# A softmax attention kernel: the exponential's [128,1] bias operand taken out, and its offset moved elsewhere

## The chip, the cores and the metric

The kernel runs on one core of one Trainium2 chip. The metric is the device time of one execution in microseconds (us); lower is better. Executions of one kernel mostly agree within 0.8%. The profile also records a granted clock, the share of its full clock that the matrix engine got. A run over 1.5% above the fastest of its kernel counts as slow and is left out of comparisons. The experiments ran on two chips, on which the kernel before took 1018.94 us (b1, a1 to a3) and 1017.3 to 1017.7 us (the rest). The engines are called as the profile calls them: PE (matrix engine; PEld is its weight loads), ACT (ScalarE), DVE (VectorE), POOL and SP.

## The reference

Two attentions over the same input are mixed by a gate. A is full softmax attention: 2048 tokens, 32 heads of 20. B looks at 8 dilated positions. The part that matters here is A's softmax:

```python
scores = jnp.einsum("bhqd,bhkd->bhqk", q, k) * scale
p = _softmax(scores, axis=-1)          # 32 heads x 2048 x 2048 exponentials
o = jnp.einsum("bhqk,bhkd->bhqd", p, v)
...
return g * a + (1 - g) * b
```

That is 134 million exponentials, by far the largest piece of elementwise work. Inputs and outputs are bfloat16.

## The kernel before

Scores come out of the matmul already scaled to "128 per octave": a score of 128 n means 2 to the n. A row of the query tile carries an offset for each query, so that the largest score of a row lies below a fixed top. Before the change that offset is 128 x (127 + TOP) with TOP = 96. The 127 is the bias of a float's exponent: VectorE builds some of the exponentials by writing integers that are read as bfloat16, and there it is wanted. ScalarE does not want it, and takes it off again with the bias of its activation, which is given as a [128,1] tile.

```python
T("dve", 0.06, lambda e: e.memset(ebias[:, :], -127.0 * LN2), writes=["ebias"])
T("dve", 0.06, lambda e: e.tensor_scalar(offs[:, :], onesrow[:, :], 128.0 * (127 + TOP), None, op0=ALU.mult), ...)
...                                             # ScalarE's way, 792 tiles of 1536 and 1024 in turn
def exp(s):
    n = len(tiles[s])                           # 3 or 2 blocks of 512 scores
    exps[s] = T("act", actc(512 * n), lambda e: e.activation(
        ebuf[s % NE][:, 0:512 * n], score[s % 2][:, 0:512 * n], ACTF.Exp, scale=LN2 / 128.0, bias=ebias[:, 0:1]),
      reads=[("score", s % 2), "ebias"], writes=[("ebuf", s % NE)])
...                                             # VectorE's way, 68 blocks of 512: four passes
T("dve", dvc(512), lambda e, b=b: e.tensor_scalar(xD[w][:, :], side[b][:, :], 16384.0, None, op0=ALU.max), ...)
T("dve", ...)  # tD = (n - 2^16) n, with n the low 16 bits of xD
T("dve", ...)  # tD = (n + H1) tD
T("dve", ...)  # eD as integers = H2 tD + xD
```

The order of all instructions is fixed when the program is built, by a planner that holds estimates of durations (`actc(n)` is 0.08 us plus 0.83 ns an element, `dvc(n)` is 0.10 us plus 1.04 ns an element). And where PE would be idle, the planner inserts matmuls whose results nobody uses ("fillers"), to keep PE's clock up:

```python
def filler(limit):
    while sch.avail["pe"] + 0.32 <= limit and sch.load(2.3) < FILL:
        ...
        T("pe", 0.215, lambda e: e.matmul(obank[:, :], zero[:, :], xT[:, 0, 0:512], start=False, stop=False, ...), ...)
```

There are two score buffers. The score matmuls of tile s may start when the exponential of tile s-2 has ended, and must be done when that of tile s-1 ends.

Of the kernel before, what the change touches and what calls it, by code (L numbers as in the profile page):

```python
# [5 lines left out]
FP32 = mybir.dt.float32  # L6
# [4 lines left out]
ALU = mybir.AluOpType  # L11
ACTF = mybir.ActivationFunctionType
AX = mybir.AxisListType

P = 128
# [12 lines left out]
SCALE = float(DH) ** -0.5  # L28
NEG = -1.0e9
TOK = 256  # L30



# [3 lines left out]
LN2 = 0.6931471805599453  # L37
OCT = 128.0 * SCALE / LN2
TOP = 96
# [175 lines left out]
def bass_gated_mix__softmax_full_mha__sliding_local_dilated__prompt_kernel(  # L215
    nc,
    A_x,
    A_wqkv,
    A_wo,
    B_x,  # L220
    B_wqkv,
    B_wo,
    gate_w,
    out,
):
    from contextlib import ExitStack

    with ExitStack() as ctx:
        _build(ctx, nc, A_x, A_wqkv, A_wo, B_wqkv, B_wo, gate_w, out)
# [10 lines left out]
def _build(ctx, nc, A_x, A_wqkv, A_wo, B_wqkv, B_wo, gate_w, out):  # L240
    sb = lambda shape, dt, name: ctx.enter_context(nc.sbuf_tensor(name, shape, dt))
# [3 lines left out]
    T = sch.task  # L245
# [3 lines left out]
    score = [ps(512 * TSZ[0], "score0"), ps(512 * TSZ[1], "score1")]  # L249
    obank = ps(512, "obank")  # L250
    side = [ps(512, "side0"), ps(512, "side1")]


    NE = 6
# [9 lines left out]
    ebuf = [sb([P, 512 * TSZ[i % 2]], BF16, "ebuf%d" % i) for i in range(NE)]  # L264
# [9 lines left out]
    xD = [gtan, gtr]  # L274
    ND = 4
    eD = sb([P, ND, 512], BF16, "eD")
    tD = sb([P, 512], FP32, "tD")
    ebias = sb([P, 1], FP32, "ebias")
    offs = sb([P, 1], FP32, "offs")
    g16 = sb([P, 16], FP32, "g16")  # L280
    tB = sb([P, TOK], FP32, "tB")
    gwT = sb([P, CN], BF16, "gwT")
# [6 lines left out]
    onesrow = sb([P, 1], FP32, "onesrow")  # L289
    qB = sb([P, CN, TOK], BF16, "qB")  # L290
    kB = sb([P, CN, TOK + PADB], BF16, "kB")
    vB = sb([P, CN, TOK + PADB], BF16, "vB")
    stage = sb([P, WIN * CN * TOK], BF16, "stage")
    eB = sb([P, 2 * TOK], BF16, "eB")
    mB = sb([P, TOK], BF16, "mB")
# [26 lines left out]
    dvc = lambda n, mode=1: 0.10 + n * 1.0417e-3 / mode  # L322
# [6 lines left out]
    def x_load(tcc, dur):  # L329
# [12 lines left out]
      writes=["WvA"], dma=True)  # L342
    T("sp", 14.0, lambda e: e.dma_start(_ap(stage, 0, [[2 * D, CN], [1, 2 * D]]), wA_v[:, :, 0:2 * D]),
      writes=["stage"], dma=True)
# [2 lines left out]

    T("pool", 0.3, lambda e: e.iota(itmp[:, :], [[1, P]], base=0, channel_multiplier=-1), writes=["itmp"])
    T("dve", 0.06, lambda e: e.memset(warm[:, :], 0.0), writes=["warm"])
    T("dve", 0.06, lambda e: e.memset(ebias[:, :], -127.0 * LN2), writes=["ebias"])  # L350
    T("act", 1.4, lambda e: e.activation(warm[:, 2:4], warm[:, 0:2], ACTF.Exp), reads=["warm"], writes=["warm2"])
    T("dve", 0.2, lambda e: e.memset(qabs[:, :], 0.0), writes=["qabs"])

# [2 lines left out]
      reads=["rB"], writes=["ident"])  # L356
    T("dve", 0.1, lambda e: e.memset(zero[:, :], 0.0), writes=["zero"])

    for i in range(7):
# [7 lines left out]
      reads=["warm"], writes=["WkP1"])  # L367
# [4 lines left out]
    for j in range(4):  # L372
        T("dve", 0.07, lambda e, j=j: e.memset(onesrow[32 * j:32 * j + 1, :], 1.0), writes=["onesrow"])
        T("dve", 0.1, lambda e, j=j: e.memset(KMmask[32 * j:32 * j + 32, 32 * j:32 * j + 1], -1.0078125),
          writes=["KMmask"])


    T("dve", 0.06, lambda e: e.tensor_scalar(offs[:, :], onesrow[:, :], 128.0 * (127 + TOP), None, op0=ALU.mult),
      reads=["onesrow"], writes=["offs"])

    def constants():
# [41 lines left out]
    def bank():  # L423
        while True:
            got = yield ("bank",)
            if got is not None:
                return got

    def release(b, t):
        bank_used[b] = False  # L430
        bank_free[b] = t.end + LAT[t.stream]
# [135 lines left out]
    def gen_d(w):  # L567


        while True:  # L570
            while lock[w] or not wanted():
                yield ("cond",)
            lock[w] = True
            b = yield from bank()
            it = yield ("ride", b)
            if it is None:
                it = lone(b)
            i, g, kb, j = it
            sl = (4 * i + j) % ND
            yield ("dve", DAHEAD)  # L580
            t = T("dve", dvc(512), lambda e, b=b: e.tensor_scalar(xD[w][:, :], side[b][:, :], 16384.0, None, op0=ALU.max),
                  reads=[("side", b)], writes=[("xD", w)])
            release(b, t)
            nn = xD[w][:, :].bitcast(U16)[:, 0:1024:2]
            while lock[2]:
                yield ("cond",)
            lock[2] = True
            yield ("dve", DAHEAD)
            T("dve", dvc(512), lambda e, nn=nn: e.scalar_tensor_tensor(tD[:, :], nn, -OCT16, nn, op0=ALU.add, op1=ALU.mult),
              reads=[("xD", w)], writes=["tD"])  # L590
            yield ("dve", DAHEAD)
            T("dve", dvc(512), lambda e, nn=nn: e.scalar_tensor_tensor(tD[:, :], nn, H1, tD[:, :], op0=ALU.add, op1=ALU.mult),  # L592
              reads=[("xD", w), "tD"], writes=["tD"])
            yield ("dve", DAHEAD)
            T("dve", dvc(512), lambda e, sl=sl: e.scalar_tensor_tensor(  # L595
                eD[:, sl, :].bitcast(I16), tD[:, :], H2, xD[w][:, :], op0=ALU.mult, op1=ALU.add),
              reads=[("xD", w), "tD"], writes=[("eD", sl)])
            lock[2] = False
            lock[w] = False
            done[("du", i, j)] = True  # L600
# [361 lines left out]
    def v_first(kb0, n, s_):  # L962
# [7 lines left out]
        for i in range(n):  # L970
# [16 lines left out]
      reads=[("side", 1)], writes=["qabs"])  # L987
# [6 lines left out]
      reads=[("kmx4", i) for i in range(4)], writes=[("kmx", 0)])  # L994
    T("dve", 0.2, lambda e: e.tensor_scalar(KM[0][:, :], KMmask[:, :], kmx[:, 0:1], None, op0=ALU.mult),
      reads=[("kmx", 0), "KMmask"], writes=[("KM", 0)])
    v_first(0, 2, 1)
    T("pe", 0.215, lambda e: e.matmul(side[1][:, :], KM[0][:, :], qabs[:, :], start=False, stop=True, skip_group_check=True),
      reads=[("KM", 0), "qabs"], accum=[("side", 1)])
    t = T("dve", dvc(512), lambda e: e.tensor_scalar(qT[0][:, :], side[1][:, :], OCT, offs[:, 0:1], op0=ALU.mult, op1=ALU.add),  # L1000
          reads=[("side", 1), "offs"], writes=[("qT", 0)])
# [29 lines left out]
    def wanted():  # L1031


        if len(dopen) > waiting[0]:
            waiting[0] += 1
            return True

        if dopen or len(dquads) > cur["pv"] or not d_time():
            return False
        t_end = sch.avail["act"]  # L1040
        for g in range(cur["g"], min(NG, cur["g"] + 2)):
            lo, hi = ahead[g]
            t_end += (4 * hi - lo - 4) * UNIT
            if done.get(("q", g)) and t_end >= sch.avail["pe"] + DTIME:
                break
        else:
            return False
        ahead[g][1] = hi - 1
        dquads.append((g, hi - 1))
        dleft[g] = dleft.get(g, 0) + 4  # L1050
        dopen.extend(range(4))
        waiting[0] += 1
        return True
# [12 lines left out]
    def lone(b):  # L1066
        it = take(dopen[0])
        i, g, kb, j = it
        q = g % NQ
        T("pe", 0.215, lambda e: e.matmul(side[b][:, :], kT[32 * j:32 * j + 32, q, kb * P:(kb + 1) * P],  # L1070
                                          qT[g % 2][32 * j:32 * j + 32, :], start=True, stop=True),
          reads=[("kT", q, kb // 4), ("qT", g % 2)], writes=[("side", b)], mode="row")
        return it
# [59 lines left out]
    def exp(s):  # L1133
        n = len(tiles[s])
        exps[s] = T("act", actc(512 * n), lambda e: e.activation(  # L1135
            ebuf[s % NE][:, 0:512 * n], score[s % 2][:, 0:512 * n], ACTF.Exp, scale=LN2 / 128.0, bias=ebias[:, 0:1]),
          reads=[("score", s % 2), "ebias"], writes=[("ebuf", s % NE)])

    def pv(units, quads):

# [91 lines left out]
    s = 0  # L1232
    while pvg < NG:
# [11 lines left out]
        if acting:  # L1245
            gn = us[-1] // 64
            run_until(("q", gn))
            if gn != g1:
                g1 = gn

                if g1 + 1 < NG:
                    if g1 + 1 < NQ:
                        add_gen(gen_k(g1 + 1), 2)
                    add_gen(gen_q(g1 + 1), 2)
                if g1 == 1:
                    add_gen(gen_v(1), 3)
                    add_gen(gen_d(0), 1.0)
                    add_gen(gen_d(1), 1.01)
                if g1 == 0:
                    add_gen(gen_gate(0), 3)  # L1260
                if g1 == 2:
                    add_gen(gen_bweights(), 4)
                if g1 % NQ == 6 and g1 // NQ + 1 < QCN:
                    add_gen(gen_gate(g1 // NQ + 1), 4)
                if g1 == 4:
                    for uu in range(2 * QCN):
                        add_gen(gen_b(uu), 6 + 0.01 * uu)
                        add_gen(gen_bproj(uu), 6.5 + 0.01 * uu)
                    add_gen(gen_prefold(), 5.5)
                    for qq in range(QCN - 1):  # L1270
                        add_gen(gen_fold(qq), 5 + 0.01 * qq)
            qk(s)
            exp(s)
# [45 lines left out]
```

## Time and profile before

| | before |
|---|---|
| median time (three runs; 1019.26 with a fourth, below) | 1019.25 us |
| ACT busy | 985.6 us of 1016.0, 97% |
| of that the 792 exponentials | 971.3 us |
| ACT idle before exponentials for late scores | 10.6 us |
| PE busy | 922.8 us, 91% |
| DVE busy | 615.1 us, 61% |

The page of the kernel before: engines' busy time, the slices of the span (a digit is tenths), the chain of waits that ended last, and groups of instructions (line, engine, operation, tiles | busy us, mean ns of one | idle us before them and what ended it).

```profile
span 1016.0 us, 16619 instructions
...
PE 922.8 (91%) x6808; PEld 316.5 (31%) x6915; DVE 615.1 (61%) x1067; ACT 985.6 (97%) x827; POOL 22.9 (2%) x20
...
ACT  5989999998999999999999999999999999999996
...
PEclk9999999998999999999999999999999999999999
...
ACT 68%; issue 21%; PE 7%; DVE 3%; DMA 1%; DVEq 0%; ACTq 0%
...
L1135 ACT ACTIVATE ebuf<-score,ebias 128x1536 bf16<-128x1536 f32 (+1 forms) x792 | 971.3, 1592 | 10.8 <-PE score L1121 10.3
L1121 PE MATMUL score<-qT,kT 32*128 32x512 bf16 x1980 | 308.5, 385 | 70.4 <-ACT ebuf L1135 39.7
...
L1121 PEld LDWEIGHTS score<-qT,kT 32*128 32x128 bf16 x1980 | 75.9, 91 | 323.0 <-ACT ebuf L1135 305.4
```

ACT is busy for 80% or more of every slice but the first and last, and the chain follows it for 68% of the span. ACT stood idle before its exponentials for 10.8 us in all, 10.6 of them in waits for scores. In the other direction, the score matmuls' weight loads waited 305.4 us for an exponential. So ScalarE is the bound. PE's 91% is a warning: it is close behind.

The mean of one exponential in the group, 1592 ns, is not its cost: an activation is counted from when it is taken up, while its predecessor still runs (below, L701 starts at 508.88 and its predecessor ends at 509.32). The cost of one is the distance between the ends of two that follow each other. The timeline of ACT shows it (start in us, length in us, instructions merged in runs of one line):

```profile
505.00 4.32 ACT L1135 ACTIVATE ebuf<-score,ebias 128x1536 bf16<-128x1536 f32 x3
508.88 0.93 ACT L701 ACTIVATE eB<-side 128x512 bf16<-128x512 f32 x1
509.35 2.89 ACT L1135 ACTIVATE ebuf<-score,ebias 128x1024 bf16<-128x1024 f32 x2
511.77 0.74 ACT L713 ACTIVATE tB<-side 128x256 f32<-128x256 f32 x1
512.03 3.92 ACT L1135 ACTIVATE ebuf<-score,ebias 128x1024 bf16<-128x1024 f32 x3
```

The first run of exponentials ends at 505.00 + 4.32 = 509.32; the exponential of L701, which has no bias, ends at 508.88 + 0.93 = 509.81, so 512 elements cost 0.49 us. The next two biased ones (1024 and 1536 elements) end at 512.24, 2.43 us later; the tanh of L713, without bias and 256 wide, 0.27 us after that. From the single records, over the whole trace, the medians are 1431 ns (1536) and 1004 ns (1024) with the bias, 487 ns (512) and 273 ns (256) without. Both fit 0.833 ns an element; the fixed part is about 152 ns with the operand and 60 ns without.

For the cost of a second operation in a VectorE instruction, groups of DVE by form:

```profile
L581 DVE TENSOR_SCALAR gtan<-side 128x512 f32<-128x512 f32 x36 | 24.8, 688 | 11.9 <-PE side L1121 11.1 <-PE side L726 0.5
...
L503 DVE TENSOR_SCALAR qT<-side,offs 128x512 bf16<-128x512 f32 x31 | 23.1, 744 | 21.7 <-PE side L445 20.7 <-PE score L1121 0.9
...
L581 DVE TENSOR_SCALAR gtr<-side 128x512 f32<-128x512 f32 x32 | 21.9, 684 | 3.2 <-PE side L1121 3.2
...
L472 DVE TENSOR_SCALAR kT<-side,onesrow 128x512 bf16<-128x512 f32 x28 | 20.8, 744 | 20.8 <-PE side L445 16.6 <-PE score L1121 4.1
```

L503 multiplies and adds, L472 adds only, both with one [128,1] operand: 744 ns both.

### The profile page before, as it was taken

The numbers are of one execution on the slowest core, as the hardware profiler recorded it, in microseconds if no ns is written. First come the engines' busy times: TensorE is split into PE (matmuls) and PEld (weight loads), VectorE is DVE, ScalarE is ACT, GpSimd is POOL, SyncE is SP. The second block draws the span as 40 slices with busy tenths as digits, with TensorE's granted clock in tenths as the row PEclk, the third lists the DMA queues.
The fourth block names the chain that finished last, engine by engine and source line by source line (L and its number), as shares of the span: only waits on it lengthen the run. The fifth ranks groups of instructions, "written<-read, shape, count | busy, mean of one in ns | idle before, by whom it ended". The sixth has DMA issues, their size and how long they took to land.

```text
span 1016.0 us, 16619 instructions
## 1 busy us (share of the span) xinstructions
PE 922.8 (91%) x6808; PEld 316.5 (31%) x6915; DVE 615.1 (61%) x1067; ACT 985.6 (97%) x827; POOL 22.9 (2%) x20
## 2 busy tenths in 40 slices
PE   6989999897999999999999899999999999998997
PEld 4323222222332323233323333333332333232222
DVE  5564577788778775861664675255358326568612
ACT  5989999998999999999999999999999999999996
POOL 0000000008000000000000000000000000000000
PEclk9999999998999999999999999999999999999999
DMA  6110000020000000000000000000000000000000
GB/s 209 39 28 1 1 1 1 1 98 1 1 2 1 2 1 1 2 7 14 7 1 1 1 2 7 14 8 1 1 1 1 7 14 8 1 1 1 1 1 27
DMA packets 9769, 13.07 MB, mean 13 GB/s; under 512 B 2397, under 2 KB 8413, under 8 KB 9693
## 3 DMA queue, kind: packets, MB, share of 16 engines
q1 hardware_dynamic: 9692, 12.00, 3.6%
q8 instruction: 54, 0.88, 0.4%
q14 instruction: 23, 0.18, 0.1%
HBM read 9.38 MB, written 2.62 MB: 12 GB/s over the span
## 4 chain that ended last, share of the span: by engine, by line
ACT 68%; issue 21%; PE 7%; DVE 3%; DMA 1%; DVEq 0%; ACTq 0%
ACT ebuf L1135 67%; PE score L1121 2%; PE side L445 2%; PE obank L1165 1%; ACT tB L713 1%; DMA oTn<-in_A_x_dram 1%; PE side L948 0%; DVE qT L503 0%; PE score L930 0%; DVE eD L595 0%; ACT eB L701 0%; DVE oTt L560 0%; DVE tD L592 0%; DVE oTt L549 0%; DVE oTn L563 0%
## 5 line engine op out<-in xcount | busy, mean ns | idle before, releaser
L1135 ACT ACTIVATE ebuf<-score,ebias 128x1536 bf16<-128x1536 f32 (+1 forms) x792 | 971.3, 1592 | 10.8 <-PE score L1121 10.3
L1121 PE MATMUL score<-qT,kT 32*128 32x512 bf16 x1980 | 308.5, 385 | 70.4 <-ACT ebuf L1135 39.7
L1165 PE MATMUL obank<-ebuf,vA 128*21 128x512 bf16 x1980 | 178.2, 386 | 1.1 <-ACT ebuf L1135 1.1
L1121 PEld LDWEIGHTS score<-qT,kT 32*128 32x128 bf16 x1980 | 75.9, 91 | 323.0 <-ACT ebuf L1135 305.4
L445 PE MATMUL side<-xT,kvw 128*128 128x256 bf16 (+1 forms) x727 | 133.0, 294 | 1.0 <-issue 0.8
L1183 PE MATMUL obank<-xT,zero 128*128 128x512 bf16 x379 | 113.8, 383 | 2.9 <-issue 2.4
L445 PEld LDWEIGHTS side<-xT,kvw 128*128 128x128 bf16 x740 | 59.0, 97 | 61.8 <-issue 43.2
L1165 PEld LDWEIGHTS obank<-ebuf,vA 128*21 128x21 bf16 x1980 | 40.1, 89 | 91.6 <-issue 85.1
L846 DVE CAST outsb<-side 128x512 bf16<-128x512 f32 (+1 forms) x24 | 11.8, 490 | 72.6 <-PE side L445 72.5
L549 DVE STREAM_TRANSPOSE oTt<-obank 128x512 f32<-128x512 f32 x32 | 22.9, 716 | 49.7 <-PE obank L1165 49.2
L738 DVE TENSOR_TENSOR stage<-vB,repB 128x1280 bf16<-128x1280 bf16 x64 | 50.4, 820 | 0.8
L1183 PEld LDWEIGHTS obank<-xT,zero 128*128 128x128 bf16 x423 | 33.6, 97 | 53.8 <-issue 37.3
L660 DVE TENSOR_TENSOR stage<-qB,kB 128x1280 bf16<-128x1280 bf16 x64 | 49.1, 818 | 0.3
L445 PE MATMUL side<-woA_r,oTn 128*128 128x128 bf16 (+1 forms) x242 | 45.5, 299 | 0.4 <-issue 0.3
L445 PE MATMUL side<-stage,ident 128*128 128x512 bf16 (+1 forms) x186 | 44.7, 346 | 0.2 <-issue 0.2
L1179 PE MATMUL side<-xT,ident 128*128 128x512 bf16 x145 | 43.6, 381 | 0.7 <-issue 0.5
L445 PE MATMUL side<-xT,WqP 128*128 128x512 bf16 x139 | 42.1, 388 | 1.9 <-issue 1.0
L751 DVE SCALAR_TENSOR_TENSOR oB<-side,rB 128x512 bf16<-128x512 f32 (+1 forms) x24 | 14.4, 600 | 42.1 <-PE side L445 40.4
L503 DVE TENSOR_SCALAR qT<-side,offs 128x512 bf16<-128x512 f32 x31 | 23.1, 744 | 21.7 <-PE side L445 20.7
L495 DVE TENSOR_SCALAR qabs<-side 128x512 uint16<-128x512 uint16 x31 | 21.0, 676 | 22.8 <-PE side L445 21.4
L472 DVE TENSOR_SCALAR kT<-side,onesrow 128x512 bf16<-128x512 f32 x28 | 20.8, 744 | 20.8 <-PE side L445 16.6
L716 DVE RECIPROCAL rB<-side 128x256 f32<-128x256 f32 x8 | 14.1, 1758 | 31.6 <-ACT tB L713 31.6
(129 smaller groups left out, 750.5 us busy)
## 6 DMA issues: line engine op xcount, KB each, us to landing
stage<-in_B_wqkv_dram SPq DMA_DIRECT2D x1, 2400.0 KB, 8.5
out_dram<-outsb SPq DMA_DIRECT2D x12, 160.0 KB, 1.8
stage<-in_A_wqkv_dram SPq DMA_DIRECT2D x1, 1600.0 KB, 11.7
oTn<-in_A_x_dram SPq DMA_DIRECT2D x2, 640.0 KB, 5.7
kvw<-in_A_wqkv_dram SPq DMA_DIRECT2D x1, 800.0 KB, 8.7
woA_r<-in_A_wo_dram SPq DMA_DIRECT2D x4, 200.0 KB
woBp<-in_B_wo_dram SPq DMA_DIRECT2D x5, 160.0 KB
oB<-in_A_x_dram SPq DMA_DIRECT2D x1, 640.0 KB, 7.6
```

What stands on the lines that cost most here:

```text
L445: ins = e.matmul(o, l, r, start=(first and i == 0), stop=(last and i == n - 1), skip_group_check=True)
L472: t = T("dve", dvc(512), lambda e, b=b, tcc=tcc: e.tensor_scalar(kT[:, q, tcc * 512:(tcc + 1) * 512], side[b][:, :], onesrow[:, 0:1], None ...
L495: T("dve", dvc(512), lambda e: e.tensor_scalar(qabs[:, :].bitcast(U16), side[b][:, :].bitcast(U16)[:, 1:1024:2], 0x7FFF, None, op0=ALU.bit ...
L503: t = T("dve", dvc(512), lambda e: e.tensor_scalar(qT[sl][:, :], side[b][:, :], OCT, offs[:, 0:1], op0=ALU.mult, op1=ALU.add), reads=[("si ...
L549: T("dve", dvc(512), lambda e: e.transpose(oTt[:, :], obank[:, :]), reads=["obank"], writes=["oTt"])
L660: TB(dvc(CN * TOK, 2), lambda e, w=w, ks=ks: e.tensor_tensor(prodB(w), qB[:, :, :], ks, ALU.mult), reads=["qB", "kB"], writes=[("prod", w) ...
L738: TB(dvc(CN * TOK, 2), lambda e, w=w, vs=vs, rr=rr: e.tensor_tensor(prodB(w), vs, rr, ALU.mult), reads=["vB", ("repB", w4 % 2)], writes=[( ...
L1121: ins = e.matmul(o, kT[32 * j:32 * j + 32, q, kb * P:(kb + 1) * P], qT[g % 2][32 * j:32 * j + 32, :], start=True, stop=True)
L1135: exps[s] = T("act", actc(512 * n), lambda e: e.activation(ebuf[s % NE][:, 0:512 * n], score[s % 2][:, 0:512 * n], ACTF.Exp, scale=LN2 / 1 ...
L1165: ins = e.matmul(obank[32 * j:32 * j + DV, :], vA[:, kb, g % NQ, j, :], src, start=(kb == 0), stop=(last and k >= len(lst) - 4), skip_grou ...
L1179: t = T("pe", 0.215, lambda e, b=b: e.matmul(side[b][:, :], ident[:, :], xT[:, 0, 0:512], start=True, stop=True), reads=["ident", ("xT", 0 ...
L1183: T("pe", 0.215, lambda e: e.matmul(obank[:, :], zero[:, :], xT[:, 0, 0:512], start=False, stop=False, skip_group_check=True), reads=["zer ...
```

## The change

The offset in the query tile loses its 127, so that ScalarE needs no bias at all. VectorE adds the 127 back in its first pass, as a second operation of the same instruction.

```diff
-    ebias = sb([P, 1], FP32, "ebias")
...
-    T("dve", 0.06, lambda e: e.memset(ebias[:, :], -127.0 * LN2), writes=["ebias"])
...
-    T("dve", 0.06, lambda e: e.tensor_scalar(offs[:, :], onesrow[:, :], 128.0 * (127 + TOP), None, op0=ALU.mult),
+    T("dve", 0.06, lambda e: e.tensor_scalar(offs[:, :], onesrow[:, :], 128.0 * TOP, None, op0=ALU.mult),
       reads=["onesrow"], writes=["offs"])
...
-            t = T("dve", dvc(512), lambda e, b=b: e.tensor_scalar(xD[w][:, :], side[b][:, :], 16384.0, None, op0=ALU.max),
+            t = T("dve", dvc(512), lambda e, b=b: e.tensor_scalar(xD[w][:, :], side[b][:, :], 128.0 * 127, 16384.0, op0=ALU.add, op1=ALU.max),
...
-            ebuf[s % NE][:, 0:512 * n], score[s % 2][:, 0:512 * n], ACTF.Exp, scale=LN2 / 128.0, bias=ebias[:, 0:1]),
-          reads=[("score", s % 2), "ebias"], writes=[("ebuf", s % NE)])
+            ebuf[s % NE][:, 0:512 * n], score[s % 2][:, 0:512 * n], ACTF.Exp, scale=LN2 / 128.0),
+          reads=[("score", s % 2)], writes=[("ebuf", s % NE)])
```

The planner's estimates are not touched, so the order of instructions on every engine is the same but for the memset.

## The prediction

> **What bounds the kernel now.** ScalarE. The page gives ACT 985.6 us busy of a span of 1016.0 (97%); from 400 to 1005 us the windows view has it busy without a gap, and the chain of waits puts 67% on the exponential alone. The exponential is 792 instructions, 971.3 us by the groups. It waited for its scores only 10.6 us in all (waits of ACT), while the score matmuls' weight loads waited for it 737 times, 305 us. PE (923 us busy, 157 us of that matmuls that only keep it warm) is close behind; DVE is at 61%.
>
> **What the change does.** It takes the [128,1] bias operand from 792 exponentials. By the distance of the ends of back-to-back instructions in the trace: biased, 1536 wide 1430 ns and 1024 wide 1004 ns, which is 0.833 ns an element plus 152 ns. Exponentials and tanhs without a bias are in the same trace: 512 wide 487 ns, 256 wide 273 ns, 0.833 ns an element plus 60 ns. So a biased one pays 91 ns more. The Trainium skill, "ScalarE: Activation LUTs", section "What ACT_TABLE_LOAD costs", says that each [128,1] pointer operand adds about 93 ns; this trace agrees, at 91. 792 x 91 = 72 us of ScalarE time go; a pair of tiles (1536 + 1024) falls from 2434 to about 2252 ns.
>
> Added: a second operation in the first of four DVE passes over VectorE's 68 tiles. I expect no cost: TENSOR_SCALAR with two operations (qT, 744 ns) takes as long as with one (kT, 744 ns), both with one pointer operand; the pass stays at 684 to 690 ns. Order, tiles given to VectorE and fillers stay.
>
> **How much lies on the critical path.** Nearly all, if PE keeps up. With two score buffers, the score matmuls of tile s start 56 ns after exponential s-2 ends (nearly all 1536-wide tiles, the median of the others), and end 557 ns (1536) or 985 ns (1024, median) before ScalarE needs them. PE's own spare time before those matmuls, median, is about 140 and 40 ns, 180 a pair: just what is taken away. I carried the trace's PE work between score matmuls forward with exponentials 91 ns shorter: the last one ends 71 us earlier, with ScalarE losing about 7 us to late scores, as before, but PE's own waiting for ScalarE falls from about 100 us to about 30. So PE becomes a near second bound, and DVE results (78% busy from 230 to 400 us) that came just in time will stall PE some more; I allow 5 us.
>
> **Prediction.** 1019 - 71 + 5 = 953 us; 8 in 10 between 944 and 970. Faster by over 2%: 0.97; within 2%: 0.025; slower: 0.005.
>
> **What would show it.** Exponentials' busy sum near 900 us; ends 1339 and 913 ns apart; ACT still 95% or more of the span; waits of the score weight loads for the exponential falling far below 305 us; ScalarE's waits for score matmuls growing from 11 to 10 to 25 us; the first DVE pass unchanged near 686 ns; PE's granted clock still 0.98 or more.
>
> **What would make it wrong.** The unbiased form may not save 91 ns at 1024 and 1536 elements; PE, near saturation, may become the bound (ACT's wait for scores of 40 us or more, most of it in 230 to 400 us or around changes of head group, where PE waits for DVE's qT); a denser PE may get a lower clock. Each would leave 965 to 985 us.

## The result

The time fell from 1019.26 us (median of 4 runs, 1018.65 to 1022.91) to 954.22 us (median of 4, 950.29 to 956.01). The ratio is 0.935, 95% interval 0.9312 to 0.9387. (Ratios here are the mean time of one kernel's fast runs over that of the other's of the same rounds, so not quite the ratio of the medians.) The prediction was 953, range 944 to 970.

The page of the changed kernel; its line numbers are one lower than before:

```profile
span 954.2 us, 16618 instructions
...
PE 904.3 (95%) x6808; PEld 317.1 (33%) x6915; DVE 612.7 (64%) x1066; ACT 918.6 (96%) x827; POOL 22.9 (2%) x20
...
ACT  5979999997999999999999999999999999999996
...
PEclk8989999998999999999999999999999999999999
...
ACT 50%; PE 31%; issue 14%; DVE 4%; DMA 1%; DVEq 0%; ACTq 0%
...
L1134 ACT ACTIVATE ebuf<-score 128x1536 bf16<-128x1536 f32 (+1 forms) x792 | 902.8, 1383 | 16.0 <-PE score L1120 14.2
L1120 PE MATMUL score<-qT,kT 32*128 32x512 bf16 x1980 | 309.7, 387 | 26.5 <-ACT ebuf L1134 11.7
...
L1120 PEld LDWEIGHTS score<-qT,kT 32*128 32x128 bf16 x1980 | 76.0, 91 | 251.6 <-ACT ebuf L1134 206.7
```

The span fell by 1016.0 - 954.2 = 61.8 us. ACT's busy time fell by 985.6 - 918.6 = 67.0, nearly all of it the exponentials' (971.3 to 902.8, 68.5), and ACT's idle time rose from 30.4 to 35.6. ACT is still 96% busy, but PE is now at 95%, and the chain of waits shows the new balance: ACT 50% where it was 68%, PE 31% where it was 7%. The score weight loads' wait for the exponential went from 305.4 to 206.7 us.

ACT's timeline, around an exponential and a tanh that never had a bias:

```profile
537.22 1.68 ACT L1134 ACTIVATE ebuf<-score 128x1536 bf16<-128x1536 f32 x1
538.57 0.82 ACT L700 ACTIVATE eB<-side 128x512 bf16<-128x512 f32 x1
539.04 2.61 ACT L1134 ACTIVATE ebuf<-score 128x1024 bf16<-128x1024 f32 x2
541.27 0.65 ACT L712 ACTIVATE tB<-side 128x256 f32<-128x256 f32 x1
541.54 2.65 ACT L1134 ACTIVATE ebuf<-score 128x1024 bf16<-128x1024 f32 x2
```

The two exponentials between them end at 541.65, 2.26 us after 539.39, where two such took 2.43 before. Over the trace the medians are 1343 ns (1536) and 917 ns (1024): 88 and 87 ns less, fixed part 63 ns. 396 x (88 + 87) ns is 69 us.

VectorE's first pass, now with two operations:

```profile
L580 DVE TENSOR_SCALAR gtan<-side 128x512 f32<-128x512 f32 x36 | 24.7, 685 | 6.7 <-PE side L1120 6.4
...
L580 DVE TENSOR_SCALAR gtr<-side 128x512 f32<-128x512 f32 x32 | 21.9, 684 | 1.3 <-PE side L1120 1.2
```

684 and 685 ns where it was 684 and 688: the added operation costs nothing.

One thing in this profile was not in the other. The granted clock of this run was 0.967: 0.949 for 445 us of it. The other three runs had 0.989 to 0.994. A second look at the same kernel (below, after_again) had no such stretch, a span of 952.8 us and nearly the same ACT figures (917.0 us busy), so the low clock made no large difference and is not part of the explanation.

### The profile page after: what moved, and what is told of

Read it like the earlier page. It is cut to its first block, busy times and chain, and to the rows that moved or that the text cites. A ratio compares the mean times of both kernels' runs of the same rounds, so it can differ in the third digit from the quotient of the medians.

```text
span 954.2 us, 16618 instructions
## 1 busy us (share of the span) xinstructions
PE 904.3 (95%) x6808; PEld 317.1 (33%) x6915; DVE 612.7 (64%) x1066; ACT 918.6 (96%) x827; POOL 22.9 (2%) x20
## 4 chain that ended last, share of the span: by engine, by line
ACT 50%; PE 31%; issue 14%; DVE 4%; DMA 1%; DVEq 0%; ACTq 0%
ACT ebuf L1134 49%; PE side L444 11%; PE score L1120 9%; PE obank L1164 5%; PE obank L1182 3%; PE side L1178 1%; PE side L947 1%; DMA oTn<-in_A_x_dram 1%; DVE eD L594 0%; DVE tD L591 0%; PE score L929 0%; ACT tB L712 0%; ACT eB L700 0%; DVE qT L502 0%; DVE tD L588 0%
## 5 line engine op out<-in xcount | busy, mean ns | idle before, releaser
L1134 ACT ACTIVATE ebuf<-score 128x1536 bf16<-128x1536 f32 (+1 forms) x792 | 902.8, 1383 | 16.0 <-PE score L1120 14.2
L1120 PEld LDWEIGHTS score<-qT,kT 32*128 32x128 bf16 x1980 | 76.0, 91 | 251.6 <-ACT ebuf L1134 206.7
L444 PE MATMUL side<-xT,kvw 128*128 128x256 bf16 (+1 forms) x727 | 135.2, 298 | 1.0 <-issue 0.8
L1182 PE MATMUL obank<-xT,zero 128*128 128x512 bf16 x379 | 115.8, 389 | 2.9 <-issue 2.4
L502 DVE TENSOR_SCALAR qT<-side,offs 128x512 bf16<-128x512 f32 x31 | 23.1, 745 | 17.3 <-PE side L444 16.5
L715 DVE RECIPROCAL rB<-side 128x256 f32<-128x256 f32 x8 | 14.1, 1758 | 27.4 <-ACT tB L712 27.4
```

What stands on the lines that cost most here:

```text
L444: ins = e.matmul(o, l, r, start=(first and i == 0), stop=(last and i == n - 1), skip_group_check=True)
L502: t = T("dve", dvc(512), lambda e: e.tensor_scalar(qT[sl][:, :], side[b][:, :], OCT, offs[:, 0:1], op0=ALU.mult, op1=ALU.add), reads=[("si ...
L1120: ins = e.matmul(o, kT[32 * j:32 * j + 32, q, kb * P:(kb + 1) * P], qT[g % 2][32 * j:32 * j + 32, :], start=True, stop=True)
L1134: exps[s] = T("act", actc(512 * n), lambda e: e.activation(ebuf[s % NE][:, 0:512 * n], score[s % 2][:, 0:512 * n], ACTF.Exp, scale=LN2 / 1 ...
```

## The experiments

Two questions were put. Is it the operand that costs, or the addition, or the numbers? And how near are the other engines to being the bound now, which decides whether the rest of a saving would still arrive? All experiments gave correct results. All times are medians of fast runs unless said otherwise.

### The bias as a constant in the instruction, nothing else changed (b1_immediate_bias)

```diff
 (kernel before)
-    ..., ACTF.Exp, scale=LN2 / 128.0, bias=ebias[:, 0:1]), reads=[("score", s % 2), "ebias"],
+    ..., ACTF.Exp, scale=LN2 / 128.0, bias=-127.0 * LN2), reads=[("score", s % 2)],
```

> The kernel before, with its bias of -127 ln 2 given as a constant in the instruction instead of as a [128,1] operand; offsets and VectorE's passes stay as before. Theory 1 (the operand's fetch is the cost, not the addition): about 954 us, ends of back-to-back exponentials 1343 and 917 ns apart. Theory 2 (adding a bias that is not zero is the cost): about 1019 us, 1431 and 1004 ns. Theory 3 (the smaller numbers or the new offsets matter): about 1019 us with short exponentials or anything between. Result correct.

Measured: 952.73 us (951.84 to 953.35), ratio 0.9338, interval 0.9302 to 0.9375; ends 1344 and 916 ns apart. The group of the exponential:

```profile
L1133 ACT ACTIVATE ebuf<-score 128x1536 bf16<-128x1536 f32 (+1 forms) x792 | 901.5, 1415 | 13.1 <-PE score L1119 12.0
```

A bias that is not zero is free when it is a constant of the instruction. This falsifies theories 2 and 3: neither the addition nor the offset's size costs anything. It also means that this one-line edit gets all of the gain; moving the offset and VectorE's second operation were not needed for it.

### A bias operand of zeros put back (a1_zero_bias_operand)

```diff
 (changed kernel)
+    ebias = sb([P, 1], FP32, "ebias");  T("dve", ..., e.memset(ebias[:, :], 0.0), ...)
-    ..., ACTF.Exp, scale=LN2 / 128.0),
+    ..., ACTF.Exp, scale=LN2 / 128.0, bias=ebias[:, 0:1]),
```

> The changed kernel with a [128,1] operand of zeros put back as the exponential's bias; all else stays changed. Theory 1: back to 1016 to 1023 us, 1431 and 1004 ns between ends. Theory 2 (a bias of zero adds nothing) and theory 3 (offsets): about 954 us.

Measured: 1019.75 us (1019.54 to 1026.02), ratio 1.001, interval 0.9967 to 1.0053; ends 1431 and 1004 ns apart, as before the change.

```profile
L1136 ACT ACTIVATE ebuf<-score,ebias 128x1536 bf16<-128x1536 f32 (+1 forms) x792 | 971.5, 1590 | 11.5 <-PE score L1122 11.0
```

Adding nothing, by way of an operand, costs the whole gain.

### The scale as an operand instead (a2_scale_operand), and both (a3_both_operands)

```diff
 (changed kernel; escale is a [128,1] tile of LN2/128, ebias one of zeros)
-    ..., ACTF.Exp, scale=LN2 / 128.0),
+    ..., ACTF.Exp, scale=escale[:, 0:1]),                          (a2)
+    ..., ACTF.Exp, scale=escale[:, 0:1], bias=ebias[:, 0:1]),      (a3)
```

> The changed kernel, no bias, but the scale given as a [128,1] operand instead of a constant. Theory 1 in its wide form (any such operand costs some 87 ns an instruction): 1016 to 1023 us, 1431 and 1004 ns. Narrow form (only the bias path costs): about 954 us.

> The changed kernel with both scale and a bias of zeros as [128,1] operands. If each is fetched in turn: another 792 x 87 ns = 69 us on top of one operand, about 1088 us, 1518 and 1091 ns between ends. If the two fetches overlap: about 1019 us.

Measured: a2 1018.83 us (1017.29 to 1020.08), ratio 0.9985, ends 1431 and 1004 ns apart. a3 1090.46 us (1088.96 to 1092.31), ratio 1.0689, ends 1522 and 1095 ns apart. The group of the exponential, a2 and then a3:

```profile
L1136 ACT ACTIVATE ebuf<-score,escale 128x1536 bf16<-128x1536 f32 (+1 forms) x792 | 971.3, 1593 | 11.1 <-PE score L1122 10.6
...
L1138 ACT ACTIVATE ebuf<-score,ebias,escale 128x1536 bf16<-128x1536 f32 (+1 forms) x792 | 1043.3, 1718 | 10.2 <-PE score L1124 10.0
```

So it is not the bias path: either [128,1] operand costs 87 or 88 ns for each instruction, and the costs of two add up (88 ns for the first at 1536 elements, 91 for the second). What the engine does in that time, no record shows. The Trainium skill, "ScalarE: Activation LUTs", section "What ACT_TABLE_LOAD costs", gives about 93 ns for each [128,1] pointer operand; these runs agree within 6 ns.

### The operand on half of the exponentials (a4_bias_operand_odd_tiles)

```diff
 (changed kernel; ebias is a [128,1] tile of zeros)
-    ..., ACTF.Exp, scale=LN2 / 128.0),
+    ..., ACTF.Exp, scale=LN2 / 128.0, bias=ebias[:, 0:1] if s % 2 else 0.0),
```

Odd tiles are the 1024-wide ones. The dependency on the ebias tile is declared for all of them.

> The changed kernel with the bias operand of zeros on the 1024-wide exponentials only, half of the 792. If ScalarE bounds the kernel all the way from the time before to the time after, the response is linear: half of the 65 us lost again, 985 to 990 us. If PE's near bound had already eaten a part of the second half of the saving, less than half comes back: 970 to 984 us.

Measured: 984.37 us (983.22 to 988.02), ratio 0.9673, interval 0.9628 to 0.9717.

```profile
L1136 ACT ACTIVATE ebuf<-score 128x1536 bf16<-128x1536 f32 x396 | 677.7, 1711 | 2.2 <-PE score L1122 2.0
L1136 ACT ACTIVATE ebuf<-score,ebias 128x1024 bf16<-128x1024 f32 x396 | 544.0, 1374 | 10.5 <-PE score L1122 9.8
```

Within this one trace the 1024-wide exponentials, with the operand, end 1004 ns apart, and the 1536-wide ones, without it, 1340. So the cost stays with the instruction that has the operand, and declaring the dependency alone costs nothing. The time is 30 us over the changed kernel (31 over after_again, which ran on the same chip) and 33 us under the kernel before in the same rounds (1017.32). The expected border between the two readings was 984 to 985, so the verdict must come from the series: no, one and two operands on each exponential gave about 953, 1019 and 1090. The first operand costs 66 us and the second 71 us of time, for 69 and 72 us of ScalarE (792 x 91 ns). The response is linear where PE has room and a few us short in the last step down. ScalarE bounds the kernel over the whole range, and PE begins to take a little of the saving at its end.

### VectorE's addition as a pass of its own (a5_add_as_own_pass)

```diff
 (changed kernel; the order on PE is unchanged)
-    t = T("dve", dvc(512), ... e.tensor_scalar(xD[w], side[b], 128.0 * 127, 16384.0, op0=ALU.add, op1=ALU.max) ...)
+    t = T("dve", dvc(512), ... e.tensor_scalar(xD[w], side[b], 128.0 * 127, None, op0=ALU.add) ...)
     release(b, t)
+    T("dve", -LAT["dve"], ... e.tensor_scalar(xD[w], xD[w], 16384.0, None, op0=ALU.max) ...)   # planned as costing nothing
```

> The changed kernel with VectorE's addition as a pass of its own (from the score bank, then the maximum in place) instead of a second operation of one pass; PE's order and the plan stay. 68 more VectorE instructions of 0.4 to 0.7 us, 27 to 47 us of VectorE time. If VectorE (64% busy) has room: within 5 us of 954. If its results come just in time between 100 and 400 us, where it is over 80% busy: 960 to 975 us, with more waits of PE for it.

Measured: 973.62 us (972.62 to 973.98), ratio 0.9558: 20 us of the gain are lost. Groups of DVE by form (L583 is the new pass), then the page's chain, then ACT's waits:

```profile
L580 DVE TENSOR_SCALAR gtan<-side 128x512 f32<-128x512 f32 x36 | 24.7, 685 | 5.6 <-PE side L1122 5.4
...
L580 DVE TENSOR_SCALAR gtr<-side 128x512 f32<-128x512 f32 x32 | 21.9, 684 | 0.6 <-PE side L1122 0.5
...
L583 DVE TENSOR_SCALAR gtan<-gtan 128x512 f32<-128x512 f32 x36 | 16.5, 459 | 1.2
...
L583 DVE TENSOR_SCALAR gtr<-gtr 128x512 f32<-128x512 f32 x32 | 14.1, 440 | 1.1
```

```profile
ACT 32%; PE 29%; DVE 28%; issue 10%; DMA 0%; DVEq 0%; ACTq 0%
```

```profile
ACT ebuf L1136 <- PE score L1122: 23.9, 24, 4.5
```

The new passes are 16.5 + 14.1 = 30.6 us of an engine that is idle over a third of the time, and yet 20 us of them reach the end. The chain shows it: DVE's share is 28% where it was 4%, and ACT's waits for score matmuls rise from 14.2 to 23.9 us. In between stands PE: its own idle time that ended on a VectorE result, summed over the waits of PE, rose from 15.0 to 29.6 us. The reading is that VectorE's passes stand in the fixed order ahead of score matmuls, by the matmuls that they feed or by the banks that they free, and where they are late, PE stops; it was not followed instruction by instruction, and the sums do not account for all of the 20 us. So folding the addition into an existing pass, at no cost, was a condition of this change as it was made.

### Narrow keep-warm matmuls (a6_short_fillers, a7_fillers_384)

```diff
 (changed kernel, same order; both kinds of filler)
-    e.matmul(obank[:, :], zero[:, :], xT[:, 0, 0:512], ...)
+    e.matmul(obank[:, 0:64], zero[:, :], xT[:, 0, 0:64], ...)      (a6; 384 in place of 64 in a7)
```

> The changed kernel with the 524 matmuls that only keep PE warm shortened from 512 to 64 columns, in the same order: about 90 us of PE time go. If the losses of some 7 us that came back after the change are PE's score matmuls coming late because PE has no spare time: 946 to 950 us, ScalarE's waits near the 11 us of before. If the fillers hold the clock: more stretches at half clock (granted clock under 0.96) and 956 us or more.

> The changed kernel with the keep-warm matmuls 384 instead of 512 columns wide, same order: 28 us of PE time less. The run with 64 columns fell to half clock for 261 us and took 1012 us. If three quarters of the filler hold the clock, the late score matmuls gain: 947 to 952 us. If the clock falls already: over 960 us.

Measured: a6 took 1013.0, 1000.48 and 1010.96 us in its three fast runs, ratio 0.9898; a fourth, slow, took 1017.32. a7's three fast runs took 950.81, 954.72 and 954.18 us, at granted clocks of 0.990 to 0.996, no different from the changed kernel; so neither reading of its expectation came: the clock held, and nothing was gained. One run of a7, the profiled one, was slow (1032.15 us, granted clock 0.747); it is not compared and its profile not used for times. Page of a6 and its ACT waits:

```profile
PE 901.3 (89%) x6843; PEld 314.4 (31%) x6915; DVE 614.1 (61%) x1066; ACT 927.2 (92%) x827; POOL 23.1 (2%) x20
...
PEclk9999977677979777699989879987999999886759
...
L1120 PE MATMUL score<-qT,kT 32*128 32x512 bf16 x1980 | 343.3, 428 | 78.6 <-ACT ebuf L1134 58.3
```

```profile
ACT ebuf L1134 <- PE score L1120: 58.6, 69, 5.1
```

Taking work away from a nearly saturated engine made the kernel 58 us slower (1010.96 against after_again's 953.07). The granted clock fell to 0.872 from 0.967 (0.992 in after_again): the clock records have 261 us at one half, against 19.5 us in the changed kernel, and score matmuls at half clock come late (ACT waits 58.6 us instead of 14.2, and 41 of the 58.6 ended in stretches at half clock, which are a quarter of the span). So the fillers cannot be cut to 64 columns. That a quarter of their width could go without any gain (a7) suggests that the fillers are not what holds up the changed kernel; a gain of 1 or 2 us would not show in three runs. The Trainium skill, "TensorE: Matmul & The Clock Gate", section "Part 1: The HAM clock gate", describes a clock that halves when PE has been idle in a window of about 3.4 us. This trace agrees in the window: the records hold stretches of 3.413 us or a multiple at exactly one half. It does not show an idle window: no gap between a6's matmuls is longer than 2.98 us. PE was still 89% busy by the profile, which books a filler of 64 columns at 205 ns on average and one of 512 at 389, so its busy time does not tell when the clock falls. Where between 64 and 384 columns the clock begins to fall was not looked for.

### The kernel before, planned for its real costs (c1_before_planned_for_bias)

```diff
 (kernel before: only the planner's estimates)
-    dvc = lambda n, mode=1: 0.10 + ...        actc = lambda n: 0.08 + ...       TOK * 7.5e-3
+    dvc = lambda n, mode=1: 0.155 + ...       actc = lambda n: 0.152 + ...      TOK * 6.87e-3
```

> The kernel before with its planner told the measured costs (152 ns fixed for an exponential with the operand, 155 ns for a VectorE pass) instead of 80 and 100 ns. Its own plan then gives VectorE 84 tiles instead of 68. If a part of what the operand cost was recoverable by planning: 1000 to 1012 us. If ScalarE's time per tile is all that counts and VectorE has no room for more tiles: 1015 us or more.

Measured: 1011.96 us (1011.26 to 1013.93), ratio 0.9939, interval 0.9904 to 0.9974. The planner had assumed 80 ns fixed for an exponential, where the operand made it 152 and its removal makes it 63. Telling it the truth recovers 5 to 6 us of the 66 that the operand costs, a small gain but clear of the noise. So the gain of the change is the operand, not a plan that happened to fit better.

### The changed kernel planned anew (c2_after_replanned_60, c3_after_replanned_64), and once more as it is (after_again)

```diff
 (changed kernel: estimates, and thresholds of the planner chosen anew; c2 / c3)
+    actc 0.064, dvc 0.155, TOK * 6.87e-3;  D0 160 / 110, BT0 215 / 230, BT1 908 / 897, BALL 223 / 216,
+    DTIME 24 / 24, DIDLE 0.5 / -0.5, FILL 0.8 / 0.85, SLACK (0.2, 0.4) / (0.3, 0.4)
```

> The changed kernel once more, unedited, beside the next three, which differ from it by about one per cent: 950 to 956 us. Its profile of the first time had a granted clock of 0.949 over 445 us; if that is a passing state of the chip it is absent here and the span is near 950 us.

> The changed kernel with its planner told the measured costs (64 ns fixed for an exponential, 155 ns for a VectorE pass) and its thresholds chosen anew for that: 60 tiles on VectorE instead of 68, planned end 936 us. If the plan with the right costs is what limits now: 935 to 944 us. If PE's density and clock limit: 948 us or more.

> The same with another choice of thresholds, 64 tiles on VectorE and 639 keep-warm matmuls instead of 575, planned end 936 us: 935 to 944 us if the plan limits; 948 us or more if PE limits.

Measured: after_again 953.07 us (951.53 to 956.72), ratio 0.936; c2 961.62 us (960.26 to 962.38), ratio 0.9439; c3 955.73 us (952.35 to 960.14), ratio 0.9388. Both plans promised 936 us and missed; c2 is worse than the unedited kernel. The reading "the plan with the right costs is what limits now" falls. c2's clock records have 34.7 us at half clock against 17.8 in after_again, and its ACT is 922.9 us busy against 917.0, since 8 blocks more are left to it; the planner knows nothing of the clock. That this is all of the difference was not shown. No experiment beat the changed kernel clearly; b1, with the simpler edit, equals it.

## Why the prediction was right

- **The bound, and the operand's cost.** Right. The estimate was 91 ns from instructions without a bias in the trace of before; measured 88 and 87. The difference of 3 to 4 ns has a likely source: those instructions stood among biased ones. In the changed kernel the same ones cost 489 and 277 ns where they cost 487 and 273 before, and a4's exponentials without the operand, each between two with it, cost 1340 where the changed kernel's cost 1343. So 69 us, not 72, left ScalarE. b1, a1, a2, a3 and a4 show that it is the operand, and neither the addition nor the offset.
- **No cost on VectorE.** Right: 684 and 685 ns. a5 shows that this mattered more than the prediction said: as a pass of its own it would have cost 20 us.
- **Nearly all of it on the critical path.** Right. Of 67.0 us of ACT's busy time, 61.8 reached the span in the first profile and 63.2 of 68.6 in after_again (1016.0 - 952.8, against 985.6 - 917.0). The exponential's waits for scores grew from 10.6 to 15.7 us; 10 to 25 had been predicted. The 5 us allowed for stalls were about what came (ACT's idle time rose by 5.2 us), but they were an allowance, not worked out, so that the sum came within 2 us of the measured time is in part luck.
- **PE as a near second bound.** Right, as far as it can be read. The time in which PE stood ready and waited only for an exponential, worked out from the single records as in the prediction, went from 95 to 16 us (20 in after_again); "about 100 to about 30" was said. The weight loads' wait fell less than "far below 305" suggests, to 206.7, for those also wait while matmuls run.
- **PE's clock at 0.98 or more.** The prediction missed it in the first profile (0.967), and met it in the others (0.989 to 0.996). It was named as a danger, and in this kernel it is one (a6), but it did not bring the time out of the range. Why one run had 0.949 over 445 us stays open.

## What to carry to other kernels

An activation that runs hundreds of times should take its scale and bias as constants of the instruction wherever they are the same for all partitions: a [128,1] operand cost some 90 ns each time here, with zeros in it as with -127 ln 2, and that was 6.5% of the kernel. Before rearranging the numbers so that a bias vanishes, try the same value as a constant. Cost such a change by the distance of the ends of back-to-back instructions, look in the same trace for instructions that already have the cheaper form, and then ask for each other engine how much of its idle time is really spare: VectorE's 36% was not, and of PE's filler time not all.

## What the Trainium skill lacked or had wrong

- "ScalarE: Activation LUTs", "What ACT_TABLE_LOAD costs": its fixed cost of 186 ns less an overlap of 93 ns makes, as an estimate, 93 ns plus 0.833 ns an element for back-to-back activations without operands. The runs show 63 plus 0.833 an element between ends (1343 and 917 ns), and 152 with one operand, where the page's figures (280 less 93) make 187. The difference that an operand makes (about 93 there, 87 to 91 here) agrees.
- "TensorE: Matmul & The Clock Gate", "Part 1: The HAM clock gate": it calls the clock binary, with a third state of 13/16 once three cores of a die are busy. This kernel uses one core, and records show 0.949 for 445 us in one run and 0.752 for 1000 of the 1030 us of one slow run (a7's profile). What the rest of the chip did is not known.
- The same section speaks of idle windows; it does not say how little work counts as idle. Here PE at 89% busy by the profile, with 575 matmuls of 64 columns among the rest (the traces with 512 columns hold records of 524 of them) and no gap over 2.98 us between matmuls, was at half clock for 261 us; with 512 columns for 19.5 us.
